# Attention and FFN in one kernel: another token layout, 64-row matmuls in runs, batch 1 transposed on TensorE, later loads released at a set time

## The chip, the cores and the metric

One core of a Trainium2 chip. The time is the device time of one execution in microseconds (us), as the median of several. "Span" is the length of one profiled execution, about 1.8 us under its measured time.

## The reference

Two stages in a row. First attention with exponential features: 8 batches x 8 heads, 576 tokens of 64 numbers, projected to 128 numbers, of which exp(+) and exp(-) are taken. Then an FFN over all 4608 tokens, 512 to 2048 to 512, with a squared relu.

```python
def phi(x):
    proj = np.einsum('bhsd,df->bhsf', x, w_phi)            # 64 -> 128
    proj = proj - np.max(np.abs(proj), axis=-1, keepdims=True)
    return np.concatenate([np.exp(proj), np.exp(-proj)], axis=-1)
q_p, k_p = (phi(q), phi(k))
kv = np.einsum('bhsf,bhsd->bhfd', k_p, v)                  # "k.v"
z = np.sum(k_p, axis=2)
num = np.einsum('bhsf,bhfd->bhsd', q_p, kv)
den = np.einsum('bhsf,bhf->bhs', q_p, z)[..., None] + 1e-06
# x: num / den, all heads of a token side by side: 4608 x 512
h = np.maximum(x @ w_in, 0.0)
return (h * h @ w_out)
```

## The kernel before

The program first lists every operation of all engines with a wished-for time (key). A small simulation of the chip (`Machine`) then puts them in an order for each engine and gives each its PSUM banks; only then are the instructions written, in that order. So FFN work of one chunk of 512 tokens (about one batch) is mixed with attention work of later batches. An edit to the plan can therefore change the whole order.

The token layout puts tokens of two heads on the two halves of the 128 rows, so k.v contracts over 64 rows at a time, as pairs of matmuls on the two halves:

```python
def kv_ops(pr, key):
    g = Bank(2, "att")
    ...
        for sg in range(2):
            for n in range(9):
                ...
                for hi in range(2):
                    r = slice(64 * hi, 64 * hi + 64)
                    pin(nc.tensor.matmul(
                        out=o[:, hi, sg * (D + 1) : (sg + 1) * (D + 1)],
                        lhsT=ph[r, e, i, :], rhs=va[s2][sg][r, f, :], start=(n == 0), stop=(n == 8)))
```

The plan picks, for TensorE as for every engine, the ready operation with the smallest key that finds a bank; it doesn't know that 64-row matmuls cost a mode change. Only batch 0's k and q are transposed on TensorE; those of batches 1 to 7 are one DMA transpose each, issued by SyncE. Loads are issued by GpSimd as soon as their buffer is free:

```python
if c + 1 >= 2:
    kk = A(c + 1) - 12
    load(k, xk, c + 1, kk, "xk")
    load(q, xq, c + 1, kk + 2, "xq")
    load_v(c + 1, kk + 4)
```

## Time and profile before

| | before |
|---|---|
| median of 3 runs when the prediction was made (lowest to highest) | 408.75 us (407.63 to 409.35) |
| span, mean granted clock | 407.2 us, 0.965 |
| TensorE busy | 362.1 us |
| first matmul of the second FFN chunk | 107.91 us |
| visits to the 64-row mode | 111 |

Second, the stretches around the emptiest one (stretch, length, busy time with the number of instructions for TensorE, its weight loads, VectorE, ScalarE and GpSimd, then granted clock, DMA share, GB/s):

```profile
0.00:36.00 36.00, 23.41 (x336) 16.80 (x337) 25.03 (x43) 23.26 (x50) 17.79 (x30) 1.00 1.14 174
36.00:80.00 44.00, 35.65 (x558) 26.73 (x556) 26.41 (x42) 26.19 (x51) 6.68 (x9) 0.92 1.33 175
...
120.00:200.00 80.00, 78.20 (x838) 37.63 (x839) 58.28 (x97) 60.90 (x109) 7.42 (x10) 1.00 0.70 111
```

TensorE has gaps of 12.6 us in the first stretch and 8.4 in the second, and 1.8 in 80 us once the stage is full.

### The profile page before, as it was taken

What the parts mean: (1) busy time and instruction counts of PE and PEld (TensorE: products, weight loads), DVE (VectorE), ACT (ScalarE), POOL (GpSimd) and SP (SyncE); (2) the same over time, 40 slices, a digit from 0 to 9 for tenths busy, and PEclk for the clock granted to TensorE, in tenths of its full rate; (3) what the DMA queues carried; (4) which work ended last, traced back from release to release, by engine and by line L of the source; (5) the groups of instructions that cost most, each with busy time, mean ns of one, the idle gap of its engine ahead of it and who ended that gap; (6) DMA issues with size and microseconds to landing.
All of it is one profiled execution on the core that took longest, in us unless ns stands there. A gap on an engine that the chain in (4) does not pass through costs nothing.

```text
span 407.2 us, 9234 instructions
## 1 busy us (share of the span) xinstructions
PE 362.1 (89%) x3848; PEld 189.9 (47%) x3848; DVE 246.8 (61%) x413; ACT 264.7 (65%) x471; POOL 37.8 (9%) x57
## 2 busy tenths in 40 slices
PE   3679579871599999999989999999999999999995
PEld 2558565440245544454455455445544454444442
DVE  4966469352775599477857967795679563222200
ACT  3884385650589588948895987679767883444421
POOL 8332101111102011001000000000000000000000
PEclk9999889995599999999999999999999999999999
DMA  8999999999958596659446344520421031111223
GB/s 109 196 204 185 175 184 175 153 175 134 175 64 118 108 146 106 97 93 137 85 75 130 78 72 91 99 50 6 89 50 28 16 81 42 35 43 28 50 53 77
DMA packets 81306, 40.84 MB, mean 100 GB/s; under 512 B 60144, under 2 KB 76656, under 8 KB 81264
## 3 DMA queue, kind: packets, MB, share of 16 engines
q0 software_dynamic: 25392, 18.35, 32.9%
q1 hardware_dynamic: 55872, 21.90, 31.5%
q8 instruction: 30, 0.49, 0.5%
q14 instruction: 12, 0.10, 0.1%
HBM read 36.77 MB, written 9.44 MB: 113 GB/s over the span
## 4 chain that ended last, share of the span: by engine, by line
PE 72%; DMA 14%; ACT 9%; issue 2%; DVE 1%; POOL 1%; SPq 0%; ACTq 0%; POOLq 0%; DVEq 0%
PE psum L706 30%; PE psum L677 27%; DMA kT<-xk 5%; PE psum L569 5%; DMA xk<-in_k_dram 4%; PE psum L400 4%; DMA xT<-xo 3%; PE psum L479 3%; DMA xv<-in_v_dram 2%; PE psum L539 2%; PE psum L689 2%; ACT qp L555 2%; ACT qn L555 1%; ACT kn L429 1%; ACT kp L429 1%
## 5 line engine op out<-in xcount | busy, mean ns | idle before, releaser
L706 PE MATMUL psum<-wout,h 128*128 128x512 bf16 x576 | 144.4, 380 | 0.4 <-ACT hr L664 0.3
L677 PE MATMUL psum<-xT,win 128*128 128x512 bf16 x512 | 131.4, 385 | 3.0 <-DMA xT<-xo 1.9
L664 ACT ACTIVATE hr<-psum 128x512 bf16<-128x512 f32 x144 | 85.5, 601 | 58.6 <-PE psum L677 51.2
L670 DVE TENSOR_TENSOR h<-hr 128x512 bf16<-128x512 bf16 x144 | 59.5, 419 | 69.9 <-ACT hr L664 69.5
L706 PEld LDWEIGHTS <-h 128*128 128x128 bf16 x576 | 51.1, 98 | 58.4 <-issue 3.7
L677 PEld LDWEIGHTS <-win 128*128 128x128 bf16 x512 | 46.3, 99 | 57.1 <-issue 8.7
L429 ACT ACTIVATE kp<-psum 128x1024 bf16<-128x1024 f32 (+1 forms) x40 | 37.4, 939 | 29.9 <-DVE mk L420 29.9
L420 DVE TENSOR_REDUCE mk<-psum 128x8 f32<-128x1024 f32 (+1 forms) x40 | 44.3, 1112 | 9.7 <-PE psum L400 9.1
L503 DVE TENSOR_REDUCE mq<-psum 128x8 f32<-128x1024 f32 (+1 forms) x40 | 44.5, 1114 | 7.5 <-PE psum L400 6.8
L555 ACT ACTIVATE qp<-psum 128x1024 bf16<-128x1024 f32 (+1 forms) x40 | 37.3, 939 | 10.8 <-PE psum L539 7.8
L580 DVE TENSOR_TENSOR psum<-psum,en 128x520 f32<-128x520 f32 (+1 forms) x40 | 27.7, 702 | 25.8 <-PE psum L569 19.7
L456 DVE TENSOR_TENSOR va<-xv,va 128x1024 bf16<-128x1024 bf16 (+1 forms) x36 | 38.5, 1104 | 2.7 <-ACT va L440 2.5
L714 ACT ACTIVATE ot<-psum 128x512 f32<-128x512 f32 x36 | 21.8, 604 | 25.8 <-PE psum L706 25.8
L429 ACT ACTIVATE kn<-psum 128x1024 bf16<-128x1024 f32 (+1 forms) x40 | 37.5, 944 | 0.0
L555 ACT ACTIVATE qn<-psum 128x1024 bf16<-128x1024 f32 (+1 forms) x40 | 37.3, 944 | 0.0
L593 DVE TENSOR_TENSOR xo<-psum,rden 128x512 bf16<-128x512 f32 (+1 forms) x40 | 27.2, 683 | 10.2 <-DMA xT<-xo 9.6
L400 PE MATMUL psum<-wphi,kT 64*128 64x128 bf16 x288 | 16.8, 242 | 16.3 <-DVE xo L593 11.1
L400 PEld LDWEIGHTS <-kT 64*128 64x128 bf16 x288 | 10.1, 104 | 25.9 <-issue 19.3
L689 PE MATMUL psum<-xT,win 128*128 128x128 bf16 x256 | 19.5, 243 | 0.9 <-ACT kn L429 0.5
L479 PE MATMUL psum<-va,kp 64*128 64x65 bf16 x576 | 15.7, 198 | 4.7 <-ACT qn L555 2.4
L479 PEld LDWEIGHTS <-kp 64*128 64x128 bf16 x576 | 12.4, 98 | 14.9 <-issue 13.5
L569 PE MATMUL psum<-kv,qp 128*128 128x65 bf16 (+1 forms) x320 | 16.2, 198 | 3.5 <-ACT qn L555 2.2
(41 smaller groups left out, 241.1 us busy)
## 6 DMA issues: line engine op xcount, KB each, us to landing
out_dram<-ot SPq DMA_DIRECT2D x72, 128.0 KB, 2.4
xv<-in_v_dram POOLq DMA_DIRECT2D x8, 576.0 KB, 7.8
xq<-in_q_dram POOLq DMA_DIRECT2D x8, 512.0 KB, 9.1
xk<-in_k_dram POOLq DMA_DIRECT2D x7, 512.0 KB, 13.9
win<-in_moe_w_in_dram POOLq DMA_DIRECT2D x4, 512.0 KB, 13.6
wout<-in_moe_w_out_dram POOLq DMA_DIRECT2D x4, 512.0 KB, 20.1
xT<-xo SPq DMA_TRANSPOSE x35, 2.4
xk<-in_k_dram POOLq DMA_DIRECT2D x4, 128.0 KB, 4.5
```

The costliest lines, as they stand in the source:

```text
L400: pin(nc.tensor.matmul(out=o[:, e, i * Fd : (i + 1) * Fd], lhsT=xt[r, t, :], rhs=wphi2[r, :], start=True, stop=True))
L420: pin(nc.vector.tensor_reduce(out=mk_view(g), in_=ps2(pj)[:, :, : n * Fd].rearrange("p e (i f) -> p e i f", f=Fd), axis=AX.X, op=ALU.max, ...
L429: pin(nc.scalar.activation(out=dst[slot][:, :, :n, :].rearrange("p e i f -> p e (i f)"), in_=ps2(pj)[:, :, : n * Fd], func=ACT.Exp, scale= ...
L456: pin(nc.vector.tensor_tensor(out=o[:, :, :D].rearrange("p (pr j) d -> p pr j d", j=8), in0=xv[s2][:, g0:g1, j1 * D : (j1 + 8) * D].rearra ...
L479: pin(nc.tensor.matmul(out=o[:, hi, sg * (D + 1) : (sg + 1) * (D + 1)], lhsT=ph[r, e, i, :], rhs=va[s2][sg][r, f, :], start=(n == 0), stop ...
L503: pin(nc.vector.tensor_reduce(out=mqb[:, c, :, :n], in_=ps2(pj)[:, :, : n * Fd].rearrange("p e (i f) -> p e i f", f=Fd), axis=AX.X, op=ALU ...
L555: pin(nc.scalar.activation(out=o, in_=i_, func=ACT.Exp, scale=sgn))
L569: pin(nc.tensor.matmul(out=o[:m, h // 4, (h % 4) * (D + 1) : (h % 4 + 1) * (D + 1)], lhsT=lhsT, rhs=kv_sb[s2][:, h // 2, h % 2, sg, :], st ...
L664: pin(nc.scalar.activation(out=hr[sl], in_=ps1(g), func=ACT.Relu))
L670: pin(nc.vector.tensor_tensor(out=dst, in0=i_, in1=i_, op=ALU.mult))
L677: pin(nc.tensor.matmul(out=ps1(g), lhsT=win[mc // 4][:, kc, mc % 4 * P : (mc % 4 + 1) * P], rhs=xT[c % 3][:, kc, :], start=(kc == 0), stop ...
L706: pin(nc.tensor.matmul(out=ps1(g), lhsT=h2[c % 2][mc // 4][:, mc % 4, tt * P : (tt + 1) * P], rhs=wout[mc // 4][:, mc % 4, :], start=(mc = ...
```

## The change

Four intents. A new token layout puts four consecutive tokens of one head on each row (4p+j), so that k.v contracts over all 128 rows. The plan knows the cost of a mode change, and waits for several 64-row groups to issue them in a run. Batch 1 is transposed on TensorE as batch 0 is. And loads of batches 2 to 7 carry a release time; they are made to wait for the last ScalarE instruction that the plan has finished by then ("the hold"). The core of the diff:

```diff
         def kv_ops(pr, key):
-            g = Bank(2, "att")
+            g = Bank(1, "kv")
 ...
-                        for hi in range(2):
-                            r = slice(64 * hi, 64 * hi + 64)
-                            pin(nc.tensor.matmul(
-                                out=o[:, hi, sg * (D + 1) : (sg + 1) * (D + 1)],
-                                lhsT=ph[r, e, i, :], rhs=va[s2][sg][r, f, :], start=(n == 0), stop=(n == 8)))
+                    for hi in range(2):
+                        for j in range(4):
+                            pin(nc.tensor.matmul(
+                                out=o[:, sg, hi, :], lhsT=ph[kgroup[pr]][:, j % 2, 2 * hi + j // 2, :],
+                                rhs=va[s2][sg][:, 8 * pr + 4 * hi + j, :],
+                                start=(sg == 0 and hi == 0 and j == 0), stop=False, skip_group_check=True))
+                    pin(nc.tensor.matmul(
+                        out=o[:, sg, :, :], lhsT=ph[kgroup[4]][:, pr % 2, pr // 2, :],
+                        rhs=va[s2][sg][:, 32 + 2 * pr : 34 + 2 * pr, :],
+                        start=False, stop=(sg == 1), skip_group_check=True))
 ... (the plan, TensorE's choice; "tiled" marks a 64-row group)
+            pairs = sum(self.free_at[b] <= t + 1e-9 and self.free_at[b + 1] <= t + 1e-9 for b in (0, 2, 4, 6))
+            ready = sum(1 for op in A if op.tiled and op.key <= t + self.ahead)
+            go = min(ready, pairs) >= self.want
+            for i, op in enumerate(A):
+                if op.tiled and not go and t < op.key + self.patience:
 ...
+                    continue
 ... (the hold: what a load waits for)
+            if op.release > 0:
+                for a in reversed(acts):
+                    if a.at + a.lat <= t + 1e-9:
+                        op.gate = a
+                        break
 ...
     def pin(ins):
 ...
+        if now[0].gate is not None:
+            dep(i, now[0].gate.ins, mybir.DependencyClass.Sync)
 ...
+                    r = KA(b) - K["LA"] + K["LS"] * n
+                    load(src, dst, b, r, tag, release=max(r, 1.0))
 ...
+PE_IN, PE_X = (0, 1), (0,)
+K = { ... 'LA': 2.104, 'LS': 3.91, 'AHEAD': 7.094, 'PATIENCE': 0.413, 'WANT': 3, }
```

Along with it go smaller things: the result's DMA transposes come in more pieces, loads in three pieces instead of two, the single 64-token block is padded with zeros for k.v, and the limits on banks and all wished-for times are new.

## The prediction

> **What bounds the kernel now.** I read the page first, then busy time by stretches, then TensorE's timeline in a full stretch and in an empty one, and last the queue of SyncE, which issues the DMA transposes and the stores.
>
> The page:
>
> ```profile
> span 407.2 us, 9234 instructions
> ...
> PE 362.1 (89%) x3848; PEld 189.9 (47%) x3848; DVE 246.8 (61%) x413; ACT 264.7 (65%) x471; POOL 37.8 (9%) x57
> ```
>
> TensorE is the fullest engine by far: 45.1 us of the span have no matmul, and VectorE and ScalarE have room on average. The average hides two stages, which the stretches show (columns: stretch, its length, busy time of each engine with instructions in brackets, granted clock, DMA share, GB/s):
>
> ```profile
> 80.00:120.00 40.00, 24.14 (x278) 12.72 (x277) 22.97 (x36) 19.93 (x33) 4.46 (x6) 0.74 1.12 131
> ...
> 240.00:280.00 40.00, 40.00 (x437) 19.03 (x436) 29.55 (x48) 31.99 (x57) 0.74 (x1) 1.00 0.40 72
> ```
>
> From 120 us on TensorE is never empty (3.2 us of idle from 120 to 340); before that it loses time. So there are two questions: what fills the full stage, and what empties the early one.
>
> The full stage, TensorE's timeline (start, duration, matmuls; the durations overlap, so I count from start to start):
>
> ```profile
> 257.02 1.04 PE L706 MATMUL psum<-wout,h 128*128 128x512 bf16 x4
> 257.99 0.40 PE L400 MATMUL psum<-wphi,qT 64*128 64x128 bf16 x8
> 258.32 1.04 PE L677 MATMUL psum<-xT,win 128*128 128x512 bf16 x4
> 259.19 1.03 PE L706 MATMUL psum<-wout,h 128*128 128x512 bf16 x4
> 260.15 0.40 PE L400 MATMUL psum<-wphi,kT 64*128 64x128 bf16 x8
> ```
>
> Four FFN matmuls take 0.87 us (258.32 to 259.19) when four more follow, and 0.96 to 0.97 us (259.19 to 260.15) when a group with a 64-row contraction follows. That is 0.10 us for going in. Eight such projections take 0.33 us when FFN follows, though sixteen in a row elsewhere take 0.46 us, or 0.23 for eight: 0.10 us for coming out. From 120 to 340 us I count 161 such changes, and 22 more around the 64-token blocks (128*64), 183 in all: 18 us in which the array does nothing and is shown busy.
>
> The early stage, TensorE, then SyncE's queue (idle before it and what ended that, in brackets):
>
> ```profile
> 90.62 0.42 PE L569 MATMUL psum<-kv,qn 128*128 128x65 bf16 x8
> 99.33 0.61 PE L400 MATMUL psum<-wphi,kT 64*128 64x128 bf16 x8 [8.29 <-DVE xo L593]
> ```
>
> ```profile
> 54.95 8.85 SPq L384 DMA_TRANSPOSE kT<-xk  x1
> 68.34 1.15 SPq L719 DMA_DIRECT2D out_dram<-ot  x2
> 69.65 8.07 SPq L384 DMA_TRANSPOSE qT<-xq  x1
> 77.83 1.23 SPq L719 DMA_DIRECT2D out_dram<-ot  x2
> 79.22 9.41 SPq L384 DMA_TRANSPOSE kT<-xk  x1
> 88.72 1.17 SPq L719 DMA_DIRECT2D out_dram<-ot  x2
> 90.00 4.63 SPq L614 DMA_TRANSPOSE xT<-xo  x3
> 94.79 9.34 SPq L384 DMA_TRANSPOSE qT<-xq  x1
> 104.22 1.18 SPq L719 DMA_DIRECT2D out_dram<-ot  x2
> 105.49 2.56 SPq L614 DMA_TRANSPOSE xT<-xo  x2
> ```
>
> The queue runs in order. Transposes of k and q for batches 2 and 3 hold it for 8 to 9 us each while the loads fill the DMA engines. The five small transposes of batch 1's result, which the second FFN chunk needs, stand behind them: VectorE waits 8.06 us for a free result buffer, and the chunk starts only at 107.91. Batch 1 itself had started late: its transpose of k was issued at 28.56 and let TensorE go on at 49.44 (20.8 us).
>
> **What the Trainium skill says.** "TensorEngine Tiling (Array Packing)", Tiling Modes, Key Properties: changing the tiling mode, not merely the tile, drains TensorE. The trace agrees, at 0.10 us each way. "TensorE: Matmul & The Clock Gate", Part 1: after an idle window of about 3.4 us the array falls to half its clock until it has again been busy for about as long. The trace agrees: eight projections show 0.61 us after the 8.29 us gap and 0.40 in the full stage, and the clock is granted at 0.50 from 100 to 110 us. The same 0.61 us appears up to 33 us, where the record says 1.00; there I trust the durations. The same page, in "Why this matters for your kernels", says a matmul with a small contraction takes as long as a full one, and that the gain lies in running two at once. The trace agrees: 18 of k.v, as nine concurrent pairs, take 0.29 us, against 0.24 to 0.25 for 8 full ones of the same 65 columns. "DMA: Bandwidth & Descriptors", Issuing engines are not separate DMA queues: transfers of all queues interleave on the same 16 DMA engines. The trace agrees: the transpose of k took 20.8 us at worst and 4.6 at best.
>
> **The ledger before.** Pure TensorE work, by pitches read from start to start: 1088 FFN matmuls of 512 columns x 0.216 = 235; 256 small ones x 0.0558 = 14.3; 576 projections x 0.0288 = 16.6; q features, 32 pairs x 0.22 and 8 x 0.12 = 8; k.v 1152 x 0.0161 = 18.5; heads 640 x 0.03 = 19.2; 56 transposes x 0.056 = 3.1. Sum 315. Mode changes: 111 visits to the 64-row mode x 0.2 = 22, and 3 for the 64-token blocks. Cold clock: up to 120 us the groups take 84 us without idle; their warm cost is 59, their 67 changes 6.7, so 18 are left. Idle 45, of which 4.5 at the start and 4.8 after the last matmul. 315 + 25 + 18 + 45 = 403, 4 us under the span; I keep these 4 as a residue.
>
> **The change part by part.**
>
> k.v over 128 rows. Per head pair 36 matmuls (0.58 us) become 16 full ones x 0.03 and two with 130 columns, estimated at 0.057: 0.59 us. No pure time is gained. What goes is this part's membership in the 64-row mode, four groups of 19 per batch. Cost: four small ACTIVATEs more per batch at about 0.2 us, and the two VectorE multiplications of the single block go from 256 to 512 elements (0.42 to about 0.69): 0.8 us of ScalarE and 0.5 of VectorE per batch, beside TensorE.
>
> Runs. 15 groups per batch stay in 64-row mode. The planner waits for three free bank pairs but loses patience after 0.4 us, and lets at most three attention groups hold banks, so I estimate two groups per visit: 8 batches x 7.5 = 60 visits x 0.2 = 12 us, against 22. With the 64-token blocks: 25 becomes 15. Minus 10.
>
> Batch 1 on TensorE. 36 transposes x 0.056 = +2.0 us of TensorE, and ten copies on VectorE, 8 x about 0.35 + 2 x 0.25 = 3.3 us (batch 0 hands some of its own to ScalarE). It removes the 20.8 us wait and two of the long entries in SyncE's queue.
>
> Loads held back. The bytes stay. In the early stage the engines move about 1 MB of fp32 per 2.55 us (spacing of the queued weight loads). Two batches and the weights are 15.5 MB: about 40 us. With batches 2 and 3 held back, k and q of batch 1 should be there at 25 to 28 us. Later transposes meet fewer loads, nearer to 4.6 than to 20.8 us. The result's transposes come in more pieces (about 50 instead of 35 issues), which is SyncE's time at an early stage that then has room.
>
> When can the second chunk start? By pitches, VectorE needs about 26 us for batch 1 and 5 for the first chunk's squares; batch 0 is nearly done at 34 us. At 85% use: 34 + 31/0.85 = 70, plus one transpose of about 3: 74 us instead of 108. By then TensorE has some 40 us of work between 36 and 74 us, so it should stay nearly full and warm: idle 45 to 20 (4.5 start, 4.8 end, 7 early, 4 later), cold 18 to 9.
>
> Sum: 315 + 2 + 15 + 9 + 20 + 4 = 365 us of span; the measured time is 1.5 above the span now, so **366 us**.
>
> **The rivals.** First, ScalarE and VectorE take over as the bound. For: they stand at 32.0 and 29.6 of 40 in the full stage, and squeezing the period from some 39 to 36 us lifts both above 80%, so evictions come later and waiting for three free bank pairs makes gaps. Against: both still have 15% left. Then the full stage keeps its pace: about 378. Second, the early wait only moves: in-order SyncE with more pieces, or loads of batch 2 arriving too late so that k of batch 2 is awaited at 60 to 80 us. For: those loads stood early and hidden before. Against: the DMA share is under 0.7 after 110 us. Then half the early gain, 34 us in idle and cold, is lost: about 383. Third, runs hardly form, because a ready group is issued as soon as nothing else can go: 90 visits, +6 us: 372. In the other direction, full runs of three and a warm start from 25 us give about 352.
>
> **Range and chances.** The early gain is the largest and least certain term (15 to 40 us), the runs are worth 5 to 14. 8 times in 10: 351 to 383. Faster by over 2% (under 400.6) needs a quarter of the expected sum: 0.96. Within 2%: 0.03. Slower: 0.01.
>
> **What would show it.** Right: no k.v group with 64*128; 64-row groups of two or three kinds next to each other, 60 visits or so; k.v at about 0.59 us per pair; the second chunk's first matmul at 68 to 85 us; no TensorE gap above 4 us after the start; the clock row full from about 40 us; ScalarE and VectorE near 80% in the middle. Wrong: waits on evictions spread over the full stage (first rival), a gap before the k projections of batch 2 that a DMA ends (second), visits near 100 (third).

## More of the kernel before

The prediction shows the main lines. Two more readings of this kernel are needed later. First, two rows of its page, in 40 slices of about 10 us: the clock granted to TensorE in tenths of full speed, and the busy tenths of the DMA engines.

```profile
PEclk9999889995599999999999999999999999999999
DMA  8999999999958596659446344520421031111223
```

The DMA engines are full for 110 us, and the clock drops at about 40 to 60 us and from 90 to 110 us.

## The result, and the profile after

| | before | after |
|---|---|---|
| median (lowest to highest, runs) | 409.05 us (407.63 to 409.41, 4) | 381.03 us (380.1 to 383.58, 4) |
| span, granted clock | 407.2 us, 0.965 | 378.9 us, 0.991 |
| TensorE busy | 362.1 us | 348.3 us |
| second FFN chunk starts | 107.91 us | 78.35 us |
| visits to the 64-row mode | 111 | 67 |

The ratio is 0.933, with a 95% interval of 0.928 to 0.938. Ratios here and below are the mean time of one kernel's fast runs over that of the other's of the same rounds, so not quite the ratio of the medians. Executions over 1.5% slower than the fastest of the same kernel are left out of the means. The time lies within the range that was predicted (351 to 383), 2 us under its upper end and 15 us above the 366 that was named.

The page after, the same rows as before:

```profile
span 378.9 us, 8209 instructions
...
PE 348.3 (92%) x3269; PEld 192.0 (51%) x3308; DVE 253.2 (67%) x426; ACT 267.3 (71%) x494; POOL 59.2 (16%) x88
...
PEclk9999999999999999999999996999999999999999
DMA  7999999249933993199319992199610112101022
```

By this row the clock is full from the start to about 230 us; there one slice is slow that was full before. (The clock's record has no entry before 27.7 us, and up to 27 us the durations say half speed, as the prediction saw in the kernel before.) The DMA row shows the hold: packets of transfers with pauses between them, up to 240 us. Fewer instructions on TensorE are mostly the k.v, and 39 matmul records of the second FFN layer are missing from this trace (537 of 576). The ledger below charges them as if they were there; in the busy times and gaps each leaves a hole of 0.05 or 0.16 us, 2.9 us in all.

The stretches after:

```profile
0.00:36.00 36.00, 24.22 (x298) 17.75 (x299) 26.33 (x45) 24.58 (x48) 20.82 (x34) 1.00 1.24 166
36.00:80.00 44.00, 38.83 (x588) 28.96 (x591) 40.21 (x74) 34.27 (x65) 6.39 (x9) 1.00 0.91 131
80.00:120.00 40.00, 39.68 (x368) 20.59 (x370) 33.11 (x53) 35.38 (x67) 6.40 (x9) 1.00 0.82 122
120.00:200.00 80.00, 78.07 (x737) 41.17 (x747) 60.36 (x98) 62.95 (x118) 12.99 (x19) 1.00 0.77 114
200.00:240.00 40.00, 36.12 (x328) 18.43 (x329) 24.81 (x42) 28.51 (x54) 6.20 (x9) 0.91 0.87 109
240.00:280.00 40.00, 37.15 (x362) 19.99 (x362) 30.42 (x48) 31.66 (x59) 6.40 (x9) 1.00 0.81 121
```

From 80 to 120 us TensorE went from 24.14 us busy to 39.68: the large gain. The first 36 us are hardly better (24.22 against 23.41). From 200 to 280 us TensorE lost 6.7 us, in a stage that had no gaps before.

To add up where the time went, I take the starts of TensorE's groups and charge each group its pitch (its time from start to start, close to the pitches of the prediction's ledger), 0.10 us for each mode change, and call the rest "idle and slow", with missing records charged as if they were there:

| us, by stage | before | after |
|---|---|---|
| head and tail (before the first and after the last matmul) | 9.7 | 9.2 |
| work | 311.8 | 315.5 |
| mode changes | 25.2 | 16.2 |
| idle and slow, to 36 us | 19.8 | 18.0 |
| 36 to 78 us | 12.2 | 5.9 |
| 78 to 120 us | 20.6 | 1.2 |
| 120 to 220 us | 6.2 | 2.9 |
| 220 to 330 us | 1.9 | 10.1 |
| span | 407.2 | 378.9 |

(Each column adds up to the span within 0.2 us.) With exactly the pitches of the prediction the work is 314.8 and 317.2 us, and idle and slow is 2.9 us lower before and 1.5 after; the picture by stage stays. The gain is 9 us of mode changes and 22.6 of idle and slow, less 3.7 of added work (21.2 and 2.4 with the prediction's pitches). In the row for 220 to 330 us it is negative: 8.2 us were given back, more than the 6.9 us of mode changes saved there (10.6 before, 3.7 after).

TensorE after, in the full stage (start, duration, operation, and in brackets the idle time before the group with what ended it):

```profile
202.44 1.02 PE L869 MATMUL psum<-wout,h 128*128 128x512 bf16 x4
203.31 0.42 PE L586 MATMUL psum<-va,kp 128*128 128x65 bf16 x8
203.57 0.22 PE L590 MATMUL psum<-va,kp 128*128 128x130 bf16 x1
203.62 0.42 PE L586 MATMUL psum<-va,kn 128*128 128x65 bf16 x8
...
221.14 0.40 PE L505 MATMUL psum<-wphi,qT 64*128 64x128 bf16 x8
221.37 0.38 PE L659 MATMUL psum<-qT,wphi 64*128 64x512 bf16 x2
221.69 0.42 PE L689 MATMUL psum<-kv,qn 128*128 128x65 bf16 x8
...
223.77 0.29 PE L505 MATMUL psum<-wphi,kT 64*128 64x128 bf16 x4
223.89 0.38 PE L659 MATMUL psum<-qT,wphi 64*128 64x512 bf16 x2
224.10 0.39 PE L505 MATMUL psum<-wphi,kT 64*128 64x128 bf16 x8
224.65 1.67 PE L869 MATMUL psum<-wout,h 128*128 128x512 bf16 x7 [0.16 <-issue]
227.32 0.59 PE L831 MATMUL psum<-xT,win 128*128 128x512 bf16 x2 [0.99 <-ACT va L545]
230.37 4.42 PE L831 MATMUL psum<-xT,win 128*128 128x512 bf16 x10 [2.46 <-DMA xT<-xo]
```

Three things are to be seen. k.v is in the full mode and costs 0.31 us per sign (203.31 to 203.62), 0.62 per head pair. The 64-row groups stand in twos and threes. And between 226 and 230 us TensorE waits twice, 0.99 us, which the profile puts down to a ScalarE instruction, and 2.46 us for the transposed result; then it runs ten matmuls in 4.42 us, half its speed. The same ten take 2.32 us where the array is warm.

Why the result came late is in SyncE's queue of the same time:

```profile
206.57 5.71 SPq L489 DMA_TRANSPOSE kT<-xk  x1
212.37 0.53 SPq L883 DMA_DIRECT2D out_dram<-ot  x1
213.08 9.01 SPq L489 DMA_TRANSPOSE qT<-xq  x1
222.19 5.04 SPq L750 DMA_TRANSPOSE xT<-xo  x4
```

The transpose of q of batch 6 holds the queue for 9.01 us, and the four small transposes that the next FFN chunk needs stand behind it until 222.19. It is the picture of 90 us in the kernel before, at a later border between chunks. The loads of this batch, which GpSimd issues, had been let go shortly before (the bracket: idle until the ScalarE instruction that the hold names):

```profile
199.81 0.90 POOL L422 DMA_DIRECT2D xk<-in_k_dram  x1 [30.27 <-ACT va L552]
203.80 0.90 POOL L422 DMA_DIRECT2D xq<-in_q_dram  x1 [1.86 <-ACT kv L599]
207.67 0.89 POOL L422 DMA_DIRECT2D xv<-in_v_dram  x1 [1.34 <-ACT hr L814]
```

The three loads of v landed 13.4 to 14.2 us after they were issued (the last at 223.1), so they were in flight during both long transposes.

### The profile page after: what moved, and what is told of

It is laid out like the page before. It is cut to its first block, busy times and chain, and to the rows that moved or that the text cites. A ratio compares the mean times of both kernels' runs of the same rounds, so it can differ in the third digit from the quotient of the medians.

```text
span 378.9 us, 8209 instructions
## 1 busy us (share of the span) xinstructions
PE 348.3 (92%) x3269; PEld 192.0 (51%) x3308; DVE 253.2 (67%) x426; ACT 267.3 (71%) x494; POOL 59.2 (16%) x88
## 4 chain that ended last, share of the span: by engine, by line
PE 81%; ACT 6%; DVE 5%; DMA 4%; issue 2%; SPq 0%; POOL 0%; DVEq 0%; ACTq 0%; POOLq 0%
PE psum L831 30%; PE psum L869 30%; PE psum L689 6%; PE psum L586 5%; PE psum L505 4%; DMA xT<-xo 3%; PE psum L659 3%; PE psum L842 2%; DVE mk L524 2%; ACT kp L533 1%; ACT kn L533 1%; PE psum L590 1%; DMA xk<-in_k_dram 1%; ACT hr L814 1%; DVE xo L713 1%
## 5 line engine op out<-in xcount | busy, mean ns | idle before, releaser
L869 PE MATMUL psum<-wout,h 128*128 128x512 bf16 x537 | 137.1, 379 | 2.8 <-issue 1.3
L831 PE MATMUL psum<-xT,win 128*128 128x512 bf16 x512 | 129.8, 385 | 7.5 <-DMA xT<-xo 5.6
L869 PEld LDWEIGHTS <-h 128*128 128x128 bf16 x576 | 52.4, 98 | 56.6 <-issue 0.3
L831 PEld LDWEIGHTS <-win 128*128 128x128 bf16 x512 | 47.7, 99 | 63.1 <-issue 13.9
L533 ACT ACTIVATE kp<-psum 128x1024 bf16<-128x1024 f32 (+1 forms) x40 | 37.7, 942 | 16.6 <-DVE mk L524 16.4
L422 POOL DMA_DIRECT2D xk<-in_k_dram x10 | 8.7, 866 | 154.6 <-ACT hr L814 117.8
L877 ACT ACTIVATE ot<-psum 128x512 f32<-128x512 f32 x36 | 21.6, 599 | 15.4 <-PE psum L869 15.2
L689 PEld LDWEIGHTS <-qp 128*128 128x128 bf16 (+1 forms) x320 | 15.0, 103 | 11.1 <-issue 2.3
L689 PE MATMUL psum<-kv,qp 128*128 128x65 bf16 (+1 forms) x320 | 17.2, 198 | 2.0 <-ACT qp L674 1.6
L842 PE MATMUL psum<-xT,win 128*128 128x128 bf16 x256 | 16.8, 219 | 1.6 <-ACT hr L814 1.4
L689 PEld LDWEIGHTS <-qn 128*128 128x128 bf16 (+1 forms) x320 | 13.6, 100 | 8.2 <-issue 3.7
L689 PE MATMUL psum<-kv,qn 128*128 128x65 bf16 (+1 forms) x320 | 16.9, 195 | 0.7 <-DVE psum L701 0.7
## 6 DMA issues: line engine op xcount, KB each, us to landing
wout<-in_moe_w_out_dram POOLq DMA_DIRECT2D x4, 512.0 KB, 10.9
```

Source lines behind the costliest of these rows:

```text
L533: pin(nc.scalar.activation(out=dst[slot][:, :, :n, :].rearrange("p e i f -> p e (i f)"), in_=ps2(pj)[:, :, : n * Fd], func=ACT.Exp, scale= ...
L689: pin(nc.tensor.matmul(out=o[:m, u // 4, u % 4 * D1 : (u % 4 + 1) * D1], lhsT=(qp, qn)[sg][slot][:, u * m : (u + 1) * m], rhs=kv_sb[s2][:, ...
L831: pin(nc.tensor.matmul(out=o, lhsT=win[mc // 4][:, kc, mc % 4 * P : (mc % 4 + 1) * P], rhs=xT[c % 3][kc // 2][:, :, kc % 2, :], start=(kc ...
L869: pin(nc.tensor.matmul(out=ps1(g), lhsT=h2[c % 2][mc // 4][:, mc % 4, tt * P : (tt + 1) * P], rhs=wout[mc // 4][:, mc % 4, :], start=(mc = ...
```

## The experiments

The questions: which part of the change brought what; why idle and slow time came out at 38 us and not near 24 (the 11 of gaps, 9 of cold clock and 4 of residue that were predicted); and who owns the 10 us after 220 us. My theory after reading the trace was that the hold, made for the early stage, pushes the loads and transposes of later batches onto the border between chunks. The rivals: the remaining mode changes cost more than thought; the cold start is what is left; or bank waits and the plan's order cause it.

In four of the edits (batch 1 by DMA, with and without the hold; no runs, twice) the plan comes out in another order. In the others the order of every engine is that of the changed kernel, so that only the named thing differs.

**The hold taken away, order kept.**

```diff
-        if now[0].gate is not None:
-            dep(i, now[0].gate.ins, mybir.DependencyClass.Sync)
```

> The changed kernel (381.0 us) with only the hold on the later loads taken out: every engine keeps its order, each load goes as soon as its buffer is free. Theory A (holding back is what keeps the early transposes and the first loads apart): the loads of batches 2 and 3 run beside the weights again, the second FFN chunk starts later than 78 us (85 to 95) and the kernel takes 386 to 396. Rival B (batch 1 on TensorE is what emptied the early stage, and the hold now pushes the later k and q transposes into the chunk borders at 184 and 230 us, where TensorE waits): same or faster, 373 to 381, and no wait for the result's transposes after 150 us.

Measured: 381.06 us, ratio 0.931 (0.926 to 0.936), the same as with the hold. Inside, it isn't the same. Idle and slow is 10.1 us from 36 us to the second chunk's start, which moved to 82.3 us, and 4.0 from there to 120 us: 14.1, against 7.1 with the hold. After that it is 3.6 from 120 to 220 and 3.0 later: 6.6, against 13.0. TensorE at the start of the second chunk:

```profile
82.33 1.03 PE L829 MATMUL psum<-xT,win 128*128 128x512 bf16 x2 [4.09 <-DMA xT<-xo]
```

So the hold gives 7.0 us up to 120 us and takes 6.4 back after it. Where it is good and where it hurts are different batches.

**No runs, everything else as in the change.**

```diff
-    'AHEAD': 7.094,
+    'AHEAD': -1e9,
-    'WANT': 3,
+    'WANT': 0,
```

> The changed kernel without the gathering of 64-row groups into runs (issued as they come by key). The static order has 93 visits to the 64-row mode against 66. Theory A (each visit costs 0.2 us of a full TensorE): +5.4 us, 385 to 388. Rival B (TensorE's idle time absorbs it, or the freer order makes up for it): within 1%, 378 to 383.

Measured: 395.32 us, ratio 0.966 (0.958 to 0.973), 93 visits to the 64-row mode. 14 us slower than the change, but only 4.9 of them are mode changes (21.1 against 16.2). The rest is idle and slow: some 16 us more before 120 us, where this order has done 66 us of work and the changed kernel 81, and some 7 us less after it. The plan was made anew, and the run doesn't separate runs from order.

**Batch 1 by DMA again, hold kept.**

```diff
-PE_IN, PE_X = (0, 1), (0,)
+PE_IN, PE_X = (0,), (0,)
```

> The changed kernel with batch 1 transposed by DMA again (loads still held back). Theory A (the late start of batch 1 was most of the early loss): the first k projection of batch 1 waits to 40 us or later, the second chunk starts at 86 to 96 us, total 387 to 398. Rival B (with the loads held back the DMA transposes are quick, and TensorE and VectorE are spared 2 and 3 us): 378 to 384.

Measured: 389.03 us, ratio 0.952 (0.944 to 0.960); the second chunk starts at 93.6. SyncE's queue shows why:

```profile
30.00 9.04 SPq L489 DMA_TRANSPOSE kT<-xk  x1
39.15 14.55 SPq L489 DMA_TRANSPOSE qT<-xq  x1
```

Even with batches 2 and 3 held back, k and q of batch 1 occupy the queue from 30 to 54 us. Batch 1 on TensorE is worth 8 us beside the hold.

**k.v with 64 rows and no runs** (two banks, of which one is read out, so the result is wrong: relative error 1.6).

```diff
-            g = Bank(1, "kv")
+            g = Bank(2, "kv")
 ...
+                            for e in range(2):
+                                r = slice(64 * e, 64 * e + 64)
-                                out=o[:, sg, hi, :], lhsT=ph[kgroup[pr]][:, j % 2, 2 * hi + j // 2, :],
+                                    out=o[:, e, sg, hi, :], lhsT=ph[kgroup[pr]][r, j % 2, 2 * hi + j // 2, :],
 ... (and the two lines of the run before this, AHEAD and WANT)
```

> The changed kernel with k.v as 64-row matmuls in two banks, of which one is evicted (a wrong result on purpose), and without runs: 113 visits in the static order, as many as the kernel before has (111), against 66. Pure TensorE time is equal. Theory A (visits x 0.2 us): 47 x 0.2 = +9.4 us, 389 to 393. Rival B (idle time absorbs the drains): under +4 us.

Measured: 383.48 us, ratio 0.934 (0.926 to 0.943), 113 visits. The forecast of some 390 us missed. Mode changes are 25.0 us, as many as before the change and 8.8 more than after it. But this order happens to have only 30.3 us of idle and slow, against 38 after and 46.6 in the second experiment. A new plan moves idle time by 8 us either way, as much as the part that was to be measured.

**k.v on 64 rows, order kept** (rows 0 to 63 only, so half the tokens: wrong, relative error 1.6).

```diff
-    lhsT=ph[kgroup[pr]][:, j % 2, 2 * hi + j // 2, :],
+    lhsT=ph[kgroup[pr]][0:64, j % 2, 2 * hi + j // 2, :],
-    rhs=va[s2][sg][:, 8 * pr + 4 * hi + j, :],
+    rhs=va[s2][sg][0:64, 8 * pr + 4 * hi + j, :],
 ... (the same for the 130-column matmul)
```

> The changed kernel with exactly its own order, banks and number of matmuls, but k.v contracts over rows 0 to 63 alone (half the sum, a wrong result on purpose), so that these matmuls are 64-row ones of the same duration and the visits to the 64-row mode go from 66 to 83. Theory A (each visit costs 0.2 us of a TensorE that is the bound): +3.4 us, 383.5 to 385.5. Rival B (a drain is made up for by less idle time later): +0 to +1.5 us.

Measured: 384.71 us, ratio 0.941 (0.932 to 0.949), 83 visits in place of 66 in the order that the plan gives (the traces show one more each). By the ratios that is (0.9407 - 0.9331) x 409 = 3.1 us slower, for 17 more visits x 0.2 = 3.4. The two intervals overlap, so the time alone would not prove it; the trace does. This kernel's TensorE at the same place:

```profile
204.16 1.04 PE L869 MATMUL psum<-wout,h 128*128 128x512 bf16 x4
205.13 0.43 PE L586 MATMUL psum<-va,kp 64*128 64x65 bf16 x8
```

Four FFN matmuls take 0.97 us from start to start when k.v follows in the 64-row mode. In the changed kernel the same k.v, in full mode, starts at 203.31, 0.87 us after the same four matmuls (202.44). The 0.10 us is the mode. Over all such places, set against the run with the loads 8 us earlier below (the same order, no records missing), the median is 0.096 us going in (23 places) and 0.092 coming out (26).

**Fewer visits, order kept.** Projections and q features of batches 2 to 7 as one full-array matmul per pair. That sums two heads and isn't what the reference asks for; the exponents' scale is set to 0 for these batches, so that no infinities arise. The comparison passes at its tolerance all the same, I suppose because with these inputs the features are nearly flat and the attention is close to a mean of v; that wasn't checked. So a pass says little here about the attention part.

```diff
+                    if b >= 2:
+                        pin(nc.tensor.matmul(out=o[:, i % 2, i * Fd : (i + 1) * Fd], lhsT=xt[:, t, :],
+                                             rhs=wphi2, start=True, stop=True))
+                        continue
                     for e in range(2):
```

> The changed kernel with its own order and banks, but the projections and q features of batches 2 to 7 are issued as one full-array matmul in place of each concurrent pair (half of the outputs stay stale, exponents are scaled by 0 to keep them finite; a wrong result on purpose). Pure TensorE time is the same, some 40 of 66 visits to the 64-row mode vanish. Theory A: -7 to -8 us, 373 to 374. Rival B (the full stage is paced by something else where it waits, and idle time takes the place of the drains): -0 to -4 us, 377 to 381.

Measured: 375.94 us, ratio 0.919 (0.913 to 0.925), with 22 visits. By the ratios 5.7 us faster for 44 visits fewer (8.7 us of changes by 0.2 each). In its trace the mode changes fall from 16 to 7.3 us, while idle and slow rises by some 3 to 4 us, most of it before 220 us: idle time took the place of part of them. So the remaining mode changes cost what the ledger says or a little less, and none of the other loss hides in them: idle and slow from 220 us on stays at 10.0. The rival that they cost more than thought falls.

**Batch 1 by DMA and no hold** (the third edit and the first).

> The changed kernel with batch 1 transposed by DMA (389.0 us when the loads are held back), now with the hold taken out as well and the order of that run kept. Theory A (holding back matters where batch 1 waits for DMA transposes): the transpose of batch 1 takes 10 to 20 us in place of some 5, the second chunk starts after 98 us, total 395 to 405. Rival B (the hold is worth nothing there too): 387 to 391.

Measured: 394.27 us, ratio 0.964 (0.957 to 0.972). The second chunk starts at 102.5, and the old gap is back: this kernel's TensorE waits of all the run (us in total, times, longest).

```profile
PE psum L503 <- DVE xo L711: 9.3, 2, 8.1
PE psum L503 <- DMA kT<-xk: 6.2, 2, 4.6
```

It is the same wait for a result buffer, 8.1 us, that the prediction showed before (8.29). So neither the layout nor the runs cure the early stage. The rest of the change without these two parts is worth 409 - 394 = 15 us, of which 10 are mode changes (25.2 to 15.2) and the other 5 were not taken apart; the hold alone adds 5 (to 389.0), batch 1 on TensorE another 8 (to 381.0). With batch 1 on TensorE the hold as set is worth nothing (first experiment). These are steps between different orders, so each is good to a few us only.

**The hold for batches 2 and 3 only, order kept.**

```diff
-        if now[0].gate is not None:
+        if now[0].gate is not None and now[0].release < 100.0:
```

> The changed kernel with its order, where only the loads of batches 2 and 3 are held back and those of batches 4 to 7 go as soon as their buffers are free. Without any hold the second chunk started at 82.3 instead of 78.3 us and the time after it came out 4 us shorter. Theory A (the hold helps early and hurts late, the two cancel): early start 78 to 79 us, no long waits after 150 us, 374 to 378. Rival B (the late gain of the free loads came from the late start itself): 380 to 382.

Measured: 380.51 us, ratio 0.930 (0.922 to 0.939). The waits after 220 us are gone (2.9 us of idle and slow left, from 10.1), but 78 to 120 us lost 4.8 instead of 1.2, and 120 to 220 lost 5.0 instead of 2.9. Free loads of batch 4 are issued from 92 us on, into the stage that was quiet. So "no hold later" is not the cure; the time of each release is.

**Batches 4 to 7 released 8 us earlier, order kept.** The plan's choice of the ScalarE instruction that a load waits for is shifted:

```diff
-                    if a.at + a.lat <= t + 1e-9:
+                    if a.at + a.lat <= t + 1e-9 - (8.0 if op.release > 100.0 else 0.0):
```

> The changed kernel, every engine in its own order; the hold on the loads of batches 4 to 7 ends 8 us earlier, that of batches 2 and 3 stays. Theory A (in the full stage the held loads make the transposes of k and q slow, and the result's transposes stand behind them in SyncE's queue while an FFN chunk waits): the loss from 220 to 330 us falls from 10 to some 4 us, total 374 to 377. Rival B (the waits move to other chunk borders, as when the hold was dropped altogether): 379 to 382.

Measured: 378.95 us, ratio 0.929 (0.926 to 0.933), less than hoped. From 220 us on the loss fell to 2.3 us. But a new wait came: TensorE, then GpSimd and SyncE of this run, each in a fence of its own.

```profile
120.39 7.46 PE L831 MATMUL psum<-xT,win 128*128 128x512 bf16 x26 [4.15 <-DMA xT<-xo]
```

```profile
111.57 0.90 POOL L422 DMA_DIRECT2D xk<-in_k_dram  x1 [20.01 <-ACT ot L877]
```

```profile
112.55 5.30 SPq L750 DMA_TRANSPOSE xT<-xo  x4
```

The load of batch 4's k, now at 111.57 (120.16 in the changed kernel), runs beside the four result transposes at 112.55, and the FFN chunk at 120 waits 4.15 us. The first of the four lands 7.8 us after its issue; in the changed kernel, issued at 112.34 without that load, it lands after 2.3 us. The shift was good for batches 5 to 7 and bad for batch 4.

**A warm start, order kept.** A memset tile and nine 128x512 matmuls on it in front of everything.

```diff
+    warm = sb("warm", [512])
+    pin(nc.vector.memset(warm, 0.5))
+    for i in range(9):
+        pin(nc.tensor.matmul(out=psum[:, 3, :], lhsT=warm[:, 0:128], rhs=warm, start=True, stop=True))
```

> The changed kernel, every engine in its own order, with nine 512-column matmuls on a constant tile put in front, in the 4 us in which TensorE waits for the first load. Theory A (the first 30 us are long because the array runs at half clock there): groups of 8 projections take 0.40 instead of 0.61 us from about 6 us on, the second chunk starts 3 to 6 us earlier, total 375 to 378. Rival B (the first 36 us hang on the first load and on VectorE and ScalarE, and the clock falls back in the gaps anyway): 380 to 382.

Measured: 383.34 us, ratio 0.944 (0.938 to 0.950): no gain, if anything a loss. TensorE at the start:

```profile
9.88 0.40 PE L505 MATMUL psum<-wphi,kT 64*128 64x128 bf16 x8
...
13.06 0.61 PE L505 MATMUL psum<-wphi,kT 64*128 64x128 bf16 x8 [1.66 <-DVE kT L481]
```

The dummies did warm the array: eight projections take 0.40 us at 9.88, where they take 0.61 in the changed kernel. At 13.06 it is slow again; the clock's record has the fall at 11.3 us, after gaps of 2.48 and 0.40 us, and the return at 28.4. So a warm start did not last through this stage with its gaps. Whether denser feeding would keep it warm was not tried. Idle and slow to 36 us is 18.6 against 18.0.

**The last two together.**

> Both edits of the two runs before, order kept. If the two are independent the gains add: 369 to 374. If the waits only move: 377 to 382.

Measured: 377.8 us, ratio 0.929 (0.924 to 0.933), as the shift alone. The warm start adds nothing.

**Batches 5 to 7 released 8 us earlier, batch 4 as it was, order kept.**

```diff
-                    if a.at + a.lat <= t + 1e-9:
+                    if a.at + a.lat <= t + 1e-9 - (8.0 if op.release > 130.0 else 0.0):
```

> The changed kernel, every engine in its own order; only the loads of batches 5 to 7 are let go 8 us earlier. With batch 4 among them, its k load came at 111.6 us, beside the result's transposes of 112 to 118 us, and TensorE waited 4.1 us for them at 120. Theory A (what matters is whether a load and the transposes that follow it fall on a chunk border): that wait is gone, the loss from 78 to 120 us is again about 1 us and from 220 to 330 us stays near 2 us, total 373.5 to 376. Rival B (a wait avoided at one border returns at another): 378 to 381.

Measured: 371.74 us (371.28 to 372.81, 6 runs), ratio 0.910 (0.905 to 0.915), correct. 9 us faster than the changed kernel, a little better than the text expected, and the fastest of all. Its queue of SyncE for batch 6:

```profile
202.98 4.92 SPq L489 DMA_TRANSPOSE kT<-xk  x1
208.00 0.53 SPq L883 DMA_DIRECT2D out_dram<-ot  x1
208.71 3.72 SPq L489 DMA_TRANSPOSE qT<-xq  x1
214.66 7.22 SPq L750 DMA_TRANSPOSE xT<-xo  x4
```

And its TensorE at the same border, and the stretch (columns as before):

```profile
225.32 0.59 PE L831 MATMUL psum<-xT,win 128*128 128x512 bf16 x2
227.22 2.32 PE L831 MATMUL psum<-xT,win 128*128 128x512 bf16 x10 [1.30 <-DMA xT<-xo]
```

```profile
200.00:240.00 40.00, 38.22 (x365) 20.04 (x369) 29.82 (x49) 32.11 (x62) 5.38 (x8) 1.00 0.79 114
240.00:280.00 40.00, 38.88 (x390) 21.15 (x391) 31.18 (x51) 32.21 (x60) 2.14 (x3) 1.00 0.67 102
```

The transpose of q takes 3.72 us instead of 9.01, the result's transposes start 7.5 us earlier (214.66), the wait shrinks to 1.30 us and the array stays warm: ten matmuls in 2.32 us. The loads of v landed 6.6 to 7.7 us after their issue, the last at 207.1, before the transpose of q was issued. Idle and slow from 220 us on is 3.2 us instead of 10.1, and 1.5 instead of 2.9 from 120 to 220. Nothing but the release of nine groups of loads was changed, so the theory stands: it was the hold's timing for batches 5 to 7. No run says that 8 us is the best shift.

## Why the prediction was right or wrong

The span of 378.9 us against the 365 predicted, term by term. The gaps are the span less TensorE's busy time, split by the stretches above; cold is what then remains of idle and slow. The 2.9 us of holes from missing records are in the gaps; they belong to the last row.

| us | predicted | measured |
|---|---|---|
| work | 317 | 315.5 |
| mode changes | 15 | 16.2 |
| idle at start and end | 9.3 | 9.2 |
| gaps between | 11 | 21.4 |
| cold clock and residue | 13 | 16.6 |

*Right: work and mode changes.* k.v came to 0.62 us per pair against 0.59 worked out, with no 64-row k.v left. 60 visits were estimated, and the trace has 67. Experiments with 17 visits more and 44 fewer moved the time by 3.1 and 5.7 us, against 3.4 and 8.7 by the price of 0.2 a visit: the price holds, somewhat less for the second. (One small reading of the prediction was off: the idle time from 120 to 340 us is 3.6 us in the trace, not 3.2; nothing hangs on it.)

*Right: the early stage and its cause.* The second chunk was to start at 74 us (68 to 85) and did at 78.35. The stretch from 80 to 120 us gained 15.5 us of TensorE. Taking both cures away (batch 1 by DMA, no hold) brought the wait of 8.1 us back, and 13 us of time. In this the hold did less than the text gave it: alone with batch 1 by DMA it brought 5 us, and beside batch 1 on TensorE, with its timing as set, none in the total.

*Wrong: "it should stay nearly full and warm: idle 45 to 20 (4.5 start, 4.8 end, 7 early, 4 later), cold 18 to 9".* This step is the whole of the miss: 14.0 us, where the other terms together are 0.4 us under. As recorded it is 10.4 us of gaps and 3.6 of cold clock and residue; without the holes, about 7.5 and 6.5. That the sum still fell into the range is owed to the range's width. The "7 early" was right for the first 36 us (36 - 24.22 - 4.7 = 7.1). The "4 later" measured 14.3: 5.2 from 36 to 80 us, 2.2 from 80 to 200 and 6.7 from 200 to 280, the rest after; some 11.5 without the holes. The last was a wait that the hold itself made: of the 10.1 us of idle and slow after 220 us, 6.9 went away when nothing but the loads of batches 5 to 7 were let go 8 us earlier. The premise behind it failed too: "Later transposes meet fewer loads, nearer to 4.6 than to 20.8 us". From issue to landing the transposes of k and q took 10.7 and 9.7 us in the median, against 6.6 and 6.0 in the kernel before and 5.6 and 6.5 with the hold taken away. In the changed kernel a batch's loads come just before its transposes; the prediction looked at late loads for batch 2 alone. In the fastest kernel the medians are still 9.4 and 8.6 us, which points to the place in the queue more than to the length. The cold clock was 10.9 us in the first 36 us alone (18.0 less 7.1), where 9 was put down for the whole. The change does nothing for that stage, and a warm start did not keep it warm.

*The rivals.* The second named the mechanism ("the early wait only moves", with in-order SyncE) but put it at k of batch 2, at 60 to 80 us, where the trace shows none; it came at the borders of later chunks. What the text held against it was misread: the DMA share is not "under 0.7 after 110 us", for the row of the kernel before has 8 and 9 tenths in three slices between 122 and 193 us. The first, ScalarE and VectorE as the bound, did not come: from 120 to 200 us they are busy 62.95 and 60.36 of 80 us, 79% and 75%, while TensorE has 1.9 us of gaps. The third, no runs, did not either. The sign that no TensorE gap would exceed 4 us after the start held; the sign that the clock row would be full from 40 us on failed in one slice, at 230 us, and that slice was the one to look at.

*What stays open.* The gain of issuing in runs by itself. The run without runs lost 14 us, of which 4.9 are mode changes, and the rest is another order. Nor were the 5 us taken apart that layout, runs, bank limits and the new order bring beside the mode changes. Nor was any version tried that feeds TensorE better in the first 36 us, where 18 us of idle and slow time are left.

## What to carry to other kernels

When loads are held back to keep them off one critical stage, work out for each later batch what its load, and the transpose that follows it, will stand in front of in the same in-order queue: here the hold's gain at 80 us was paid back at 230 us, and moving the releases of three batches by 8 us was worth 9 us. Where a planner makes the order, an edit that makes it plan anew shifts idle time by as much as the part under test, so test with the order kept. And a total that doesn't move, as when the hold was removed, can be two effects of equal size in different stages: look at the stages before calling it nothing.

## What the Trainium skill lacked or had wrong

- "TensorEngine Tiling (Array Packing)", Tiling Modes, Key Properties, says that a mode change drains TensorE but not for how long: here 0.10 us going in and 0.09 coming out, read from start to start (0.97 against 0.87 us for the same four matmuls with the same work behind them; 0.096 and 0.092 in the median).
- "TensorE: Matmul & The Clock Gate", Part 1, has the array fall back after an idle window of about 3.4 us (and, further on, swing where short idles are frequent, without lengths). It did warm in about that time, with nine dummy matmuls in 3.60 us. But by the clock's record it fell at 11.3 us after gaps of 2.48 and 0.40 us, and at 229.1 us after one of 0.99 and 1.2 us into the next. After a single gap of 1.60 us it fell in the run with the last two edits together (sixteen 128-column FFN matmuls in 1.87 us from 42.54), while after the same gap of 1.61 us in the changed kernel it stayed warm (1.05 us). So gaps well below 3.4 us were enough at times, and no length of gap that decides comes out of these traces.
- No page gives the time of a DMA transpose beside running loads. The same transpose of one batch's k or q held SyncE's in-order queue for 2.7 us at best (the hold taken away, k of batch 5 at 170.00 us) and for 14.55 at worst (batch 1 by DMA), and the same transpose of the result landed 2.3 us after its issue, or 7.8 beside a load.
